# A Fourier filter and gated convolution on one core: TensorE pieces in halves of the array instead of quarters, the first input loaded whole, and a new order

## The chip, the cores and the metric

The kernel runs on one NeuronCore of a Trainium2 chip. The metric is the device time of one execution in microseconds (us). Work is done by TensorE (PE in the profile; its loads of stationary operands are the row PEld), VectorE (DVE), ScalarE (ACT) and GpSimd (POOL); SyncE (SP) and, for a few transfers at the start, ScalarE's queue issue the DMAs.

## The reference

Eight sequences x[b] of 3200 positions with 256 channels, all float32. What is computed, cut to what matters:

```python
X = np.fft.rfft(x, axis=1)                       # along the 3200 positions
Yr = Xr @ w_r - Xi @ w_i + b_r                   # complex 256x256 mix of the channels
Yi = Xr @ w_i + Xi @ w_r + b_i
Yr, Yi = soft_threshold(Yr, 0.01), soft_threshold(Yi, 0.01)
y = np.fft.irfft(Yr + 1j * Yi, n=3200, axis=1)
gate = sigmoid(sum(conv_w[k] * shifted(y, K - 1 - k) for k in range(5)))   # causal, per channel
out = (gate * (y @ w_val)) @ w_out
```

## The kernel before, in words

The transform of 3200 points is split into 64 x 50. For each of the eight sequences (`b`) there are three groups of stages.

- **First transform** (`p1`; for b = 0 `p1_first`): eight pieces `u`. A piece multiplies 50 rows of input, four quadrant matmuls of 512 columns, by the constant `f1`. Two vector operations make sum and difference, and the result goes to DRAM (`a_dram`) and comes back transposed by the load of `a`.
- **Spectrum** (`p2`, six per sequence, and `p2_last`): `s2` on TensorE (the "columns": the loaded data `a` are the stationary operand and the constant `f2`, 64 columns, streams), then casts into a high and a low part (`xs`), `mix_sum` and `mix` (float32r matmuls with 128 x 128 weights, tiles `k_ps` and `y_ps`), the threshold, and `s1i`, the first step of the transform back (`back`: constant `g1` stationary, 256 columns stream, tile `z_ps`), stored to DRAM (`z_dram`).
- **Positions and gate** (`positions`, eight per sequence): `zl` comes back from `z_dram`, `s2i` is the last step of the transform back (`zl` stationary, constant `g2` of 50 columns streams, tile `y_p`). Then `gated`: five taps of the convolution on DVE (tile `acc`), sigmoid, and the products with `w_val` (`v_ps`) and `w_out` (`o_ps`).

The three steps that the change touches are the fp32 matmuls with 64 or 50 contracted rows. Each is one call in the source and two instruction pairs in the profile (a load and a matmul, twice). The loops over `i` or `h` take the upper and the lower 64 rows of the array, and the loop over `e` takes the left and the right 64 columns: so four 64 x 64 quarters work side by side. `s2` is line 729, `s1i` line 633 and `s2i` line 819. In the profile a piece of `s2` has 64 matmul instructions (16 in each quarter), a piece of `s2i` 64 (16 in each quarter) and a piece of `s1i` 32 (8 in each quarter). There are 48, 64 and 48 such pieces.

The order of all instructions is laid out in advance on the host. `Plan.add` (line 102) takes a piece with a due key `at`, its engine and its cost in ns; `Plan.order` (line 121) plays an event model of engines, buffers (`SLOTS`), one DMA wire (`WIRE`, `BACKLOG`, `kb`) and semaphore lanes, and among the pieces that could start next on an engine takes the one with the smallest key. The offsets between stages are the numbers in `O`. Each engine then runs its instructions strictly in that order. Adjacent quarter pieces are favoured (`together`), since a change of the kind of matmul has a cost there (`SWITCH`).

At the start `p1_loads` (line 489) brings the first sequence: rows 0 to 47 of each half as one to two pieces wide, 192 or 384 KB a transfer, half 0 on SP's queue and half 1 on ACT's; rows 48 and 49 as transfers of one row each, cut in 16; the eighth piece by itself (200 KB for each half). Behind them on SP's queue come the biases, `w_r`, `w_i` and the first part of `f2` (lines 975 to 978 and 446), and behind these the stores of the first transform (`a_dram`, line 546). TensorE runs matmuls on zeros (`warm`, line 965) while it waits.

Of the kernel before, what the change touches and what calls it, by code (L numbers as in the profile page):

```python
# [18 lines left out]
P = 128  # L19
HP = P // 2  # L20
# [206 lines left out]
WIRE = 230  # L227
BACKLOG = 5000
# [7 lines left out]
def act(n, kind="copy"):  # L236
# [6 lines left out]
O = {'hold': -35.796,  # L243
     'together': 179.833,
     'later': 15.783,
     'load_x': 185.007,
     'p1': 53.805,
     'p1_step': 1.225,
     'load_a': -102.613,
     's2': -151.326,  # L250
     's1i': -39.149,
     'p3': -53.371,
     'load_z': 236.25,
     'y': 129.884,
     'conv': 171.164,
     'val': 58.845,
     'gate': 58.043,
     'project': 12.753,
     'late_val': 7.079,
     'late_out': 15.503,  # L260
     'turn': 289.535,
     'mix_sum': -73.595,
     'p1_1': -216.196,
     'load_x_1': 9.338,
     'p1_2': -26.917,
     'p3_0': -4.777}
# [9 lines left out]
def fourier_filter_then_gated_conv(ctx: ExitStack, tc: tile.TileContext, x, w_r, w_i, b_r, b_i,  # L276
# [57 lines left out]
    def load_matrix(at, name, w, dst):  # L334
        key = ("st", name)
        n = 2 * D

        def load():
            st = room(key, "o", n).rearrange("p (j d) -> p j d", j=2)
            nc.sync.dma_start(out=st, in_=w.rearrange("(j p) d -> p j d", p=P))  # L340
# [81 lines left out]
    def load_f2(at, part):  # L422
        t = slice(F2_PARTS[part] * P, F2_PARTS[part + 1] * P)
        add(at, "SP", 400, lambda: nc.sync.dma_start(out=f2_sb[:, t], in_=f2[:, t]), STORED if part else (), [("f2", part, 0)],
            kb=(t.stop - t.start) / 2)
# [12 lines left out]
    def load_bias(at):  # L438
        key = ("st", "bias")
        st = lambda: tl[key][0:1, 0:2 * D]  # L440

        def load():
            room(key, "yb", 2 * D)
            for k, b in enumerate((b_r, b_i)):
                nc.sync.dma_start(out=st()[:, k * D:(k + 1) * D], in_=b.rearrange("(o d) -> o d", o=1))
        add(-91, "SP", 800, load, (), [key + (0,)], {key: "yb"}, kb=20)

        def marks():
            nc.gpsimd.memset(f32(ones), 1.0)
# [5 lines left out]
        add(at, "ACT", act(2 * D, "cast"), lambda: nc.scalar.copy(out=rows[0:1], in_=st()), [key + (0,)], [("bias", 0, 0)])  # L455
        add(at + 0.01, "DVE", dve(2 * D), lambda: nc.vector.tensor_tensor(
            out=rows[32:33], in0=st(), in1=f32(rows[0:1]), op=ALU.subtract), [key + (0,)], [("bias", 0, 0)])
# [31 lines left out]
    def p1_loads():  # L489

        src = x[0].rearrange("(n h m) c -> h n (m c)", h=NH, m=NM)
        wide = y_sb.rearrange("p c h n -> p (c h n)")[:, 0:7 * 4 * D]
        queue = (("SP", nc.sync), ("ACT", nc.scalar))
        n = N2 - 2
        k7 = ("x", (0, 7))

        def rows(h, lo, hi):
            queue[h][1].dma_start(out=wide[h * HP:h * HP + n, lo * 4 * D:hi * 4 * D], in_=src[h, 0:n, lo * 4 * D:hi * 4 * D])

        def row(h, r):  # L500
            queue[h][1].dma_start(out=wide[h * HP + r:h * HP + r + 1, :].rearrange("p (a n) -> p a n", a=16),
                                  in_=src[h, r:r + 1, 0:7 * 4 * D].rearrange("p (a n) -> p a n", a=16))

        def single(h):
            xt = tl[k7] if h else room(k7, "x", 4 * D)
            queue[h][1].dma_start(out=xt[half(h), :], in_=src[h, :, 7 * 4 * D:])
        for i, (lo, hi) in enumerate(((0, 1), (1, 3), (3, 5), (5, 7))):
            for h in range(NH):
                add(-100 + 2 * i, queue[h][0], 400, lambda h=h, lo=lo, hi=hi: rows(h, lo, hi), (), [("x", (0, u), h) for u in range(lo, hi)], kb=130 * (hi - lo))
            if i == 0:  # L510
                for r in (n, n + 1):
                    for h in range(NH):
                        add(-99.9, queue[h][0], 400, lambda h=h, r=r: row(h, r), (), [("x_rows", (0, r), h)], kb=20)
        for h in range(NH):
            add(-93, queue[h][0], 400, lambda h=h: single(h), (), [k7 + (h,)], None if h else {k7: "x"}, kb=200)

    def p1_first(u, at):
# [29 lines left out]
        rows = [("x_rows", (0, r), h) for r in (N2 - 2, N2 - 1) for h in range(NH)] if u < 7 else []  # L547
        add(at, "PE", 890, products, [kx + (h,) for h in range(NH)] + [("f1", 0, 0), *rows], [kp + (0,), ("turn", "p1", u)], {kp: "ps_2"}, mode="q")
# [4 lines left out]
        for k in range(2):  # L553
            add(at + 0.02, "SP", 400, lambda k=k: store(k), [ks + (0,), ks + (1,)], [("a_dram", 0, (u, k)), ("stored", 0, (u, k))],
                {("a_dram", 0): "a_dram"} if (u, k) == (0, 0) else None, kb=160)

    def p1(b, u, at):
# [36 lines left out]
        add(at + O["load_x"] + O["load_x_1"] * (b == 1), "SP", 700, load, STORED if b == 1 else (), [kx + (0,)], {kx: "x"}, kb=330, chain="x", moves=2)  # L594
# [4 lines left out]
        add(at + 0.02, "SP", 1500, store, [ks + (0,), ks + (1,)], [ka + (u,)], {ka: "a_dram"} if u == 0 else None, kb=330, moves=2)  # L599
# [16 lines left out]
    def back(b, us, at, last=False):  # L616
# [5 lines left out]
        def s1i():  # L622
            p = two_banks(kz)
            if last:
                nc.tensor.matmul(p[:, 0, 0:D], g1_sb[:, 2 * us[0] * P:(2 * us[0] + 1) * P], tl[kts[0]][:, 0, :], start=True, stop=True)
                return
            for j, v in enumerate(us):
                g = g1_sb[:, 2 * v * P:(2 * v + 2) * P].rearrange("p (r q) -> p r q", r=2)

                for r in range(2):  # L630
                    for i in range(2):
                        for e in range(2):
                            nc.tensor.matmul(p[e * HP:(e + 1) * HP, i, j * D:(j + 1) * D],  # L633
                                             g[i * HP:(i + 1) * HP, r, e * HP:(e + 1) * HP],
                                             tl[kts[j]][i * HP:(i + 1) * HP, r, :], start=r == 0, stop=r == 1)
# [11 lines left out]
        def store():  # L647
# [7 lines left out]
            kb=90 * nz)  # L655
# [50 lines left out]
    def p2(b, v, at):  # L706
# [9 lines left out]
        add(at + O["load_a"], "SP", 800, load, stored_a(b), [ka + (0,)], {ka: "a"}, kb=360, chain="a", moves=2)  # L716


        def s2():
            p = buffer(k2, "ps_s2", [P, 2, 512]).rearrange("p i (j c r h k) -> p i j c r h k", j=2, c=2, r=2, h=2)  # L720
            for j, u in enumerate(us):
                for h in range(NH):
                    f = f2_sb[:, (2 * u + h) * HP:(2 * u + h + 1) * HP]
                    for c in range(2):
                        for i in range(2):
                            rows = slice(i * HP, (i + 1) * HP)
                            for e in range(2):
                                lo = c * P + e * HP
                                nc.tensor.matmul(p[e * HP:(e + 1) * HP, i, j, c, :, h, :], tl[ka][rows, h, j, lo:lo + HP],  # L729
                                                 f[rows], start=True, stop=True)  # L730
        add(at + O["s2"], "PE", 990, s2, [ka + (0,), f2_key(us[0]), f2_key(us[1])], [k2 + (0,)], {k2: "ps_s2"}, mode="q")
# [63 lines left out]
    def positions(b, k, at):  # L795
# [14 lines left out]
        def s2i():  # L810
# [4 lines left out]
            for c in range(2):  # L815
                for m in range(MB):
                    for h in range(NH):
                        for e in range(2):
                            nc.tensor.matmul(pv[h][e * HP:(e + 1) * HP, c, m, :],  # L819
                                             zt[half(h), m, c * P + e * HP:c * P + (e + 1) * HP], g2_sb[half(h), :],  # L820
                                             start=True, stop=True)
# [65 lines left out]
    def gated(b, k, at):  # L887
# [42 lines left out]
        if bk == (B - 1, NB - 1):  # L930
# [10 lines left out]
        add(kind, "SP", 400, lambda: nc.sync.dma_start(out=dst, in_=tl[ko]), [ko + (0,)], (), kb=280)  # L941
# [106 lines left out]
```

## Time and profile before

| | |
|---|---|
| median of 3 runs | 920.74 us (917.67 to 924.05) |
| the profiled execution | 926.22 us, span of its instructions 924.4 us |
| mean granted TensorE clock | 0.978 |
| TensorE matmul / weight loads busy | 868.5 us (94%) / 726.7 us (79%) |
| VectorE / ScalarE busy | 767.1 us (83%) / 591.4 us (64%) |
| DMA | 165.14 MB, mean 179 GB/s |

In rows of groups the columns are: line, engine, operation, tiles (out<-in), shape, count | busy time in us, mean ns of one | idle time of the engine just before it, with what ended it. A shape such as `64*64 64x256` is a stationary operand of 64 rows and 64 columns and 256 streamed columns. In rows of the timeline they are: start and length in us, engine, line, operation, tiles, count, and in brackets the idle time before. Ends of matmuls are modelled, so the rate of matmuls is read from their starts. "issue" is time in which an engine waited for nothing that the profile shows.

### The profile page before, as it was taken

To read this page: it belongs to the slowest core of one execution; us is meant where nothing else is said; L and a number is where in the kernel's file an instruction comes from. 1 tells how busy PE (TensorE), PEld (TensorE's weight loads), DVE (VectorE), ACT (ScalarE), POOL (GpSimd) and SP (SyncE) were. 2 spreads that over 40 slices of the span, in tenths; PEclk is the share of its full clock that TensorE was granted. 3 is DMA by queue.
4 is the path that set the end of the run, shared out by engine and by line. 5 is a ranking of instruction groups with operands and counts; after the bars stand their busy time and mean duration, and the time that the engine had idled before them with its cause. 6 is when DMAs were issued, how large, how long until landed. Compare 5 with 4: busy or idle time off the path is not lost.

```text
span 924.4 us, 29210 instructions
## 1 busy us (share of the span) xinstructions
PE 868.5 (94%) x12846; PEld 726.7 (79%) x12846; DVE 767.1 (83%) x1016; ACT 591.4 (64%) x867; POOL 5.6 (1%) x13
## 2 busy tenths in 40 slices
PE   6889889999999999899999999899999999899888
PEld 2357668879888798779878888688988998798665
DVE  1547897999889998699969998889969996798686
ACT  1235566776577776567667766576777777676553
POOL 0000000000000000000000000001000000000000
PEclk7999999999999999799999999899999999999999
DMA  7678787766464956565566475546552445323512
GB/s 142 211 233 277 245 264 235 263 202 186 130 193 145 300 175 192 164 212 176 185 222 208 144 240 183 162 166 203 163 168 98 146 143 156 110 77 117 169 54 89
DMA packets 105442, 165.14 MB, mean 179 GB/s; under 512 B 9946, under 2 KB 78172, under 8 KB 105024
## 3 DMA queue, kind: packets, MB, share of 16 engines
q1 hardware_dynamic: 104996, 161.64, 55.3%
q10 hardware_dynamic: 320, 1.64, 1.0%
q8 instruction: 101, 1.65, 0.8%
q14 instruction: 25, 0.20, 0.1%
HBM read 83.55 MB, written 79.69 MB: 177 GB/s over the span
## 4 chain that ended last, share of the span: by engine, by line
PE 67%; DVE 19%; DMA 6%; issue 5%; ACT 3%; SPq 0%; ACTq 0%; DVEq 0%
PE y_ps L768 11%; PE o_ps L851 11%; PE v_ps L851 10%; PE z_ps L633 7%; PE y_p L819 6%; PE k_ps L773 6%; DVE acc L873 6%; PE s L729 5%; PE p L572 4%; PE y_ps L766 3%; DMA zl<-z_dram 2%; DMA y_sb<-in_x 2%; PE warm L965 2%; DVE acc L915 2%; DVE gated L330 1%
## 5 line engine op out<-in xcount | busy, mean ns | idle before, releaser
L873 DVE SCALAR_TENSOR_TENSOR acc<-y_sb,cw_sb,acc 128x800 f32<-128x800 f32 (+1 forms) x264 | 259.5, 1022 | 5.6 <-ACT acc L870 4.8
L768 PE MATMUL y_ps<-w_sb,xs 128*128 128x256 f32 x1152 | 165.3, 283 | 1.0 <-issue 1.0
L851 PE MATMUL o_ps<-gated,wo_sb 128*128 128x400 f32 x756 | 152.7, 351 | 1.5 <-DVE s L585 0.8
L768 PEld LDWEIGHTS y_ps<-w_sb,xs 128*128 128x128 f32 x1152 | 152.3, 192 | 1.2 <-issue 1.1
L851 PEld LDWEIGHTS o_ps<-gated,wo_sb 128*128 128x128 f32 x756 | 136.3, 190 | 7.7 <-issue 2.0
L851 PE MATMUL v_ps<-y_hl,wv_sb 128*128 128x400 f32 x660 | 130.3, 346 | 0.5 <-ACT o L939 0.5
L851 PEld LDWEIGHTS v_ps<-y_hl,wv_sb 128*128 128x128 f32 x660 | 117.8, 188 | 1.9 <-ACT o L939 1.4
L773 PEld LDWEIGHTS k_ps<-w_sb,xs 128*128 128x128 f32 x576 | 75.7, 190 | 27.3 <-issue 15.9
L633 PE MATMUL z_ps<-tp,g_sb 64*64 64x256 f32 x1536 | 94.5, 380 | 1.3 <-issue 1.2
L773 PE MATMUL k_ps<-w_sb,xs 128*128 128x256 f32 x576 | 91.3, 294 | 1.1 <-issue 1.1
L819 PE MATMUL y_p<-g_sb,zl 50*64 50x50 f32 x4096 | 76.7, 223 | 15.8 <-issue 13.6
L819 PEld LDWEIGHTS y_p<-g_sb,zl 50*64 50x64 f32 x4096 | 69.6, 137 | 21.1 <-issue 13.5
L610 ACT ACTIVATE tp<-yb,nlam 128x512 f32<-128x512 f32 x96 | 69.8, 729 | 19.8 <-DVE yb L780 19.7
L939 ACT COPY o<-o_ps 128x800 f32<-128x800 f32 x63 | 52.0, 826 | 43.9 <-PE o_ps L851 43.1
L780 DVE TENSOR_TENSOR yb<-y_ps,kc 128x512 f32<-128x512 f32 x96 | 65.6, 683 | 17.1 <-PE y_ps L768 17.0
L328 ACT CAST gated<-acc 128x800 fp32r<-128x800 f32 x63 | 54.2, 861 | 37.6 <-DVE acc L915 37.3
L612 DVE SCALAR_TENSOR_TENSOR tp<-yb,tp 128x512 f32<-128x512 f32 x96 | 65.4, 683 | 15.4 <-ACT tp L610 15.2
L633 PEld LDWEIGHTS z_ps<-tp,g_sb 64*64 64x64 f32 x1536 | 56.8, 133 | 25.0 <-issue 6.0
L915 DVE TENSOR_TENSOR acc<-v_ps,acc 128x800 f32<-128x800 f32 x64 | 62.8, 983 | 8.3 <-PE v_ps L847 4.2
L330 DVE TENSOR_TENSOR gated<-acc,gated 128x800 fp32r<-128x800 f32 x63 | 62.0, 984 | 8.4 <-ACT gated L328 8.3
L766 PE MATMUL y_ps<-bias_rows,ones 128*128 128x256 f32 x192 | 59.4, 309 | 10.1 <-DVE yb L780 6.6
L330 DVE TENSOR_TENSOR y_hl<-y_sb,y_hl 128x800 fp32r<-128x800 f32 x55 | 54.0, 984 | 16.1 <-ACT y_hl L328 16.1
(87 smaller groups left out, 1106.6 us busy)
## 6 DMA issues: line engine op xcount, KB each, us to landing
a_dram<-s SPq DMA_DIRECT2D x128, 208.0 KB
zl<-z_dram SPq DMA_DIRECT2D x128, 200.0 KB
out<-o SPq DMA_DIRECT2D x63, 400.0 KB
a<-a_dram SPq DMA_DIRECT2D x96, 256.0 KB
z_dram<-z_t SPq DMA_DIRECT2D x48, 512.0 KB
x<-in_x SPq DMA_DIRECT2D x96, 208.0 KB
x<-in_x SPq DMA_DIRECT2D x17, 200.0 KB
y_sb<-in_x ACTq DMA_DIRECT2D x3, 384.0 KB
```

What stands on the lines that cost most here:

```text
L330: add(at + 0.001, "DVE", dve(n), lambda: nc.vector.tensor_tensor(out=low(), in0=src(), in1=f32(high()), op=ALU.subtract), [*uses, hl[0]], ...
L610: nc.scalar.activation(out=buffer(kt, "tp", [P, 2, D])[:, 0:n], in_=tl[kb][:, 0:n], func=AF.Relu, bias=nlam)
L612: add(at + 0.2, "DVE", dve(n * D), lambda: nc.vector.scalar_tensor_tensor(out=tl[kt][:, 0:n], in0=tl[kb][:, 0:n], scalar=LAM, in1=tl[kt][: ...
L633: nc.tensor.matmul(p[e * HP:(e + 1) * HP, i, j * D:(j + 1) * D], g[i * HP:(i + 1) * HP, r, e * HP:(e + 1) * HP], tl[kts[j]][i * HP:(i + 1) ...
L766: nc.tensor.matmul(p[:, 1 - r, :], ones, rows[:, (1 - r) * D:(2 - r) * D], start=True, stop=False)
L768: nc.tensor.matmul(p[:, 1 - r, :], xm(hx, j, c, r), w_sb[:, m, hw, c, :], start=False, stop=k == 5)
L773: nc.tensor.matmul(p, sm(hx, j, c), w_sb[:, 0, hw, c, :], start=k == 0, stop=k == 5)
L780: add(atu + 0.2, "DVE", dve(2 * D), lambda ky=ky, kb=kb, kc=kc: nc.vector.tensor_tensor(out=buffer(kb, "yb", [P, 2, D]), in0=tl[ky], in1=t ...
L819: nc.tensor.matmul(pv[h][e * HP:(e + 1) * HP, c, m, :], zt[half(h), m, c * P + e * HP:c * P + (e + 1) * HP], g2_sb[half(h), :], start=True ...
L851: nc.tensor.matmul(p[:, e, 0:TB], w[:, hw, c, e * P:(e + 1) * P], src(hy, c), start=n == 0, stop=n == 5)
L873: nc.vector.scalar_tensor_tensor(out=acc(c), in0=y_of(c, j), scalar=cw_sb[:, c, j:j + 1], in1=acc(c), op0=ALU.mult, op1=ALU.add)
L915: add(at + O["gate"], "DVE", dve(2 * TB), lambda: nc.vector.tensor_tensor(out=gate(), in0=hn(tl[kv][:, :, 0:TB]), in1=gate(), op=ALU.mult) ...
```

## The change

1. `s2`, `s1i` and `s2i` lose the loop over `e`: an instruction takes 64 (or 50) rows and all 128 columns, two row halves work side by side in place of four quarters, and there are half as many instructions (32, 32 and 16 a piece in place of 64, 64 and 32).
2. The first input is loaded in 16 transfers of 50 rows, 200 KB each, one for each piece and half; three of them on ACT's queue and 13 on SP's. The transfers of single rows go.
3. `w_r`, `w_i`, the biases and the first part of `f2` are moved behind the first transform's pieces on SP's queue (keys -24 to -20 and -27 in place of -90 to -88 and -91).
4. The model's costs (`WIRE`, `BACKLOG`, `kb`, `extra`, and 900 and 850 ns for `s2` and `s2i` in place of 990 and 950) and all offsets in `O` are other numbers, so that the order of all instructions is another.

```diff
-WIRE = 230
-BACKLOG = 5000
+WIRE = 210
+BACKLOG = 4000
...
-O = {'hold': -35.796,
-     'together': 179.833,
-     'later': 15.783,
-     'load_x': 185.007,
+O = {'hold': -6.037,
+     'together': 302.016,
+     'later': -48.45,
+     'load_x': 138.371,
...
-        add(-91, "SP", 800, load, (), [key + (0,)], {key: "yb"}, kb=20)
+        add(-27, "SP", 800, load, (), [key + (0,)], {key: "yb"}, kb=20, moves=2)
...
-        for i, (lo, hi) in enumerate(((0, 1), (1, 3), (3, 5), (5, 7))):
-            for h in range(NH):
-                add(-100 + 2 * i, queue[h][0], 400, lambda h=h, lo=lo, hi=hi: rows(h, lo, hi), (), [("x", (0, u), h) for u in range(lo, hi)], kb=130 * (hi - lo))
...
+        def load(u, h):
+            dst = wide[:, u * 4 * D:(u + 1) * 4 * D] if u < 7 else tl[k7] if h else room(k7, "x", 4 * D)
+            queue[h and u < 3][1].dma_start(out=dst[half(h), :], in_=src[h, :, u * 4 * D:(u + 1) * 4 * D])
+        for u in range(8):
             for h in range(NH):
+                add(-100 + u, queue[h and u < 3][0], 400, lambda u=u, h=h: load(u, h), (), [("x", (0, u), h)],
+                    {k7: "x"} if (u, h) == (7, 0) else None, kb=200)
...
-                        for e in range(2):
-                            nc.tensor.matmul(p[e * HP:(e + 1) * HP, i, j * D:(j + 1) * D],
-                                             g[i * HP:(i + 1) * HP, r, e * HP:(e + 1) * HP],
-                                             tl[kts[j]][i * HP:(i + 1) * HP, r, :], start=r == 0, stop=r == 1)
+                        nc.tensor.matmul(p[:, i, j * D:(j + 1) * D], g[i * HP:(i + 1) * HP, r, :],
+                                         tl[kts[j]][i * HP:(i + 1) * HP, r, :], start=r == 0, stop=r == 1)
...
-                            for e in range(2):
-                                lo = c * P + e * HP
-                                nc.tensor.matmul(p[e * HP:(e + 1) * HP, i, j, c, :, h, :], tl[ka][rows, h, j, lo:lo + HP],
-                                                 f[rows], start=True, stop=True)
-        add(at + O["s2"], "PE", 990, s2, [ka + (0,), f2_key(us[0]), f2_key(us[1])], [k2 + (0,)], {k2: "ps_s2"}, mode="q")
+                            nc.tensor.matmul(p[:, i, j, c, :, h, :], tl[ka][rows, h, j, c * P:(c + 1) * P],
+                                             f[rows], start=True, stop=True)
+        add(at + O["s2"], "PE", 900, s2, [ka + (0,), f2_key(us[0]), f2_key(us[1])], [k2 + (0,)], {k2: "ps_s2"}, mode="q")
...
-                        for e in range(2):
-                            nc.tensor.matmul(pv[h][e * HP:(e + 1) * HP, c, m, :],
-                                             zt[half(h), m, c * P + e * HP:c * P + (e + 1) * HP], g2_sb[half(h), :],
-                                             start=True, stop=True)
+                        nc.tensor.matmul(pv[h][:, c, m, :], zt[half(h), m, c * P:(c + 1) * P], g2_sb[half(h), :], start=True, stop=True)
...
-    load_matrix(-90, "w_r", w_r, w_sb[:, 0])
-    load_matrix(-89, "w_i", w_i, w_sb[:, 1])
-    sums(-88.9)
-    load_f2(-88, 0)
+    load_matrix(-24, "w_r", w_r, w_sb[:, 0])
+    load_matrix(-23.5, "w_i", w_i, w_sb[:, 1])
+    sums(-23)
+    load_f2(-20, 0)
     load_bias(-30)
```

More of the change, by code (lines that the diff above doesn't have):

```diff
@@ L242 @@
 T = float(NU)
-O = {'hold': -35.796,
-     'together': 179.833,
-     'later': 15.783,
-     'load_x': 185.007,
[L247 to L258, printed above, removed]
+O = {'hold': -6.037,
+     'together': 302.016,
+     'later': -48.45,
+     'load_x': 138.371,
+     'p1': 48.724,
+     'p1_step': 0.649,
+     'load_a': -101.487,
+     's2': -99.512,
+     's1i': -24.78,
+     'p3': -63.063,
+     'load_z': 121.656,
+     'y': 164.631,
+     'conv': 195.971,
+     'val': 69.272,
+     'gate': -140.59,
+     'project': 9.897,
      'late_val': 7.079,
      'late_out': 15.503,
[L261 to L266, printed above, removed]
+     'turn': 255.513,
+     'mix_sum': -0.111,
+     'p1_1': -220.218,
+     'load_x_1': 30.986,
+     'p1_2': -29.144,
+     'p3_0': 1.769}
 WARM = 6, 1, 1, 1, 1, 1, 1, 1, 14
@@ L340, in load @@
             nc.sync.dma_start(out=st, in_=w.rearrange("(j p) d -> p j d", p=P))
-        add(at, "SP", 400, load, (), [key + (0,)], {key: "o"}, kb=256)
+        add(at, "SP", 400, load, (), [key + (0,)], {key: "o"}, kb=160)
         v = lambda: tl[key][:, 0:n].rearrange("p (j d) -> p j d", j=2)
@@ L432, in load_g1 @@
         add(at, "SP", 400, lambda: nc.sync.dma_start(out=g1_sb[:, t], in_=g1[:, t]), STORED, [("g1", part, 0)],
-            kb=(t.stop - t.start) / 2)
+            kb=(t.stop - t.start) / 3.2)
     def g1_key(u):
@@ L546, in store @@
             nc.sync.dma_start(out=dst[:, :, lo:lo + 512], in_=st()[k * HP:k * HP + NF])
-        rows = [("x_rows", (0, r), h) for r in (N2 - 2, N2 - 1) for h in range(NH)] if u < 7 else []
-        add(at, "PE", 890, products, [kx + (h,) for h in range(NH)] + [("f1", 0, 0), *rows], [kp + (0,), ("turn", "p1", u)], {kp: "ps_2"}, mode="q")
+        add(at, "PE", 890, products, [kx + (h,) for h in range(NH)] + [("f1", 0, 0)], [kp + (0,), ("turn", "p1", u)], {kp: "ps_2"}, mode="q")
         first = lambda h: [START[h]] if u == 7 else []
@@ L554, in p1_first @@
             add(at + 0.02, "SP", 400, lambda k=k: store(k), [ks + (0,), ks + (1,)], [("a_dram", 0, (u, k)), ("stored", 0, (u, k))],
-                {("a_dram", 0): "a_dram"} if (u, k) == (0, 0) else None, kb=160)
+                {("a_dram", 0): "a_dram"} if (u, k) == (0, 0) else None, kb=160, extra=-300)
     def p1(b, u, at):
@@ L593, in store @@
                 nc.sync.dma_start(out=dst[:, :, lo:lo + 512], in_=st()[k * HP:k * HP + NF])
-        add(at + O["load_x"] + O["load_x_1"] * (b == 1), "SP", 700, load, STORED if b == 1 else (), [kx + (0,)], {kx: "x"}, kb=330, chain="x", moves=2)
+        add(at + O["load_x"] + O["load_x_1"] * (b == 1), "SP", 700, load, STORED if b == 1 else (), [kx + (0,)], {kx: "x"}, kb=320, chain="x", moves=2)
         add(at, "PE", 890, products, [kx + (0,), ("f1", 0, 0)], [kp + (0,)], {kp: "ps_2"}, mode="q")
@@ L598, in p1 @@
         add(at + 0.011, "DVE", dve(512), difference, [kp + (0,), ks + ("turned",)], [ks + (1,)])
-        add(at + 0.02, "SP", 1500, store, [ks + (0,), ks + (1,)], [ka + (u,)], {ka: "a_dram"} if u == 0 else None, kb=330, moves=2)
+        add(at + 0.02, "SP", 1500, store, [ks + (0,), ks + (1,)], [ka + (u,)], {ka: "a_dram"} if u == 0 else None, kb=320, moves=2, extra=-300)
     HL = ((0, 0), (0, 1), (1, 0))
@@ L715, in load @@
                 nc.sync.dma_start(out=at_[:, h], in_=src.rearrange("(j r) c -> r j c", r=P))
-        add(at + O["load_a"], "SP", 800, load, stored_a(b), [ka + (0,)], {ka: "a"}, kb=360, chain="a", moves=2)
+        add(at + O["load_a"], "SP", 800, load, stored_a(b), [ka + (0,)], {ka: "a"}, kb=320, chain="a", moves=2)
         def s2():
@@ L936, in gated @@
                     {ko: "o"} if e == 0 else None)
-                add(kind, "SP", 400, lambda e=e: nc.sync.dma_start(out=dst[:, e], in_=tl[ko][:, e]), [ko + (e,)], (), kb=140)
+                add(kind, "SP", 400, lambda e=e: nc.sync.dma_start(out=dst[:, e], in_=tl[ko][:, e]), [ko + (e,)], (), kb=125, extra=-900)
             return
@@ L940, in gated @@
             [kp + (0,), kp + (1,)], [ko + (0,)], {ko: "o"})
-        add(kind, "SP", 400, lambda: nc.sync.dma_start(out=dst, in_=tl[ko]), [ko + (0,)], (), kb=280)
+        add(kind, "SP", 400, lambda: nc.sync.dma_start(out=dst, in_=tl[ko]), [ko + (0,)], (), kb=250, extra=-900)
     def late_weights(at):
```

20 lines of the change are left out of this document (3 added, 17 removed).

## The prediction

> **What bounds the kernel now.** I read the page's busy times first, then the busy time by stage, to see where an engine has room.
>
> ```profile
> span 924.4 us, 29210 instructions
> PE 868.5 (94%) x12846; PEld 726.7 (79%) x12846; DVE 767.1 (83%) x1016; ACT 591.4 (64%) x867; POOL 5.6 (1%) x13
> ...
> PE 67%; DVE 19%; DMA 6%; issue 5%; ACT 3%; SPq 0%; ACTq 0%; DVEq 0%
> ```
>
> ```profile
> core 0: us, PE busy (x) PEld busy (x) DVE busy (x) ACT busy (x) POOL busy (x), PEclk, DMA share, GB/s
> 0.00:51.00 51.00, 38.98 (x118) 13.60 (x118) 15.65 (x24) 8.63 (x14) 1.83 (x11) 0.87 0.73 188
> 51.00:882.00 831.00, 794.34 (x12591) 688.29 (x12591) 719.16 (x951) 562.73 (x826) 3.79 (x2) 0.98 0.58 183
> 882.00:924.00 42.00, 35.18 (x140) 24.85 (x138) 32.27 (x42) 20.05 (x29) 0.00 (x0) 1.00 0.21 78
> ```
>
> All pieces that the change recuts run between 51 and 882 us. There TensorE is busy 794.3 of 831 us: it has 36.7 us to spare, and two thirds of the chain of waits is PE. What a recut piece gains or loses on PE therefore mostly reaches the end. How much of these three lines lies on the chain, its split by line tells:
>
> ```profile
> by line: PE y_ps L768 10.8%; PE o_ps L851 10.7%; PE v_ps L851 9.8%; PE z_ps L633 7.2%; PE y_p L819 6.2%; PE k_ps L773 6.0%; DVE acc L873 5.8%; issue 4.6%; PE s L729 4.5%; PE p L572 3.8%; PE y_ps L766 2.5%; DMA zl<-z_dram 2.3%; DMA y_sb<-in_
> ```
>
> **What a piece costs now.** Six groups (matmuls and loads), and one stretch of PE's timeline in which three kinds follow each other without a gap:
>
> ```profile
> L633 PE MATMUL z_ps<-tp,g_sb 64*64 64x256 f32 x1536 | 94.5, 380 | 1.3 <-issue 1.2
> L819 PE MATMUL y_p<-g_sb,zl 50*64 50x50 f32 x4096 | 76.7, 223 | 15.8 <-issue 13.6 <-DMA zl<-z_dram 1.3 <-DVE s L585 0.4
> L819 PEld LDWEIGHTS y_p<-g_sb,zl 50*64 50x64 f32 x4096 | 69.6, 137 | 21.1 <-issue 13.5 <-DMA zl<-z_dram 1.7 <-ACT y_sb L826 0.7
> L729 PE MATMUL s<-f_sb,a 64*64 64x64 f32 x3072 | 56.5, 222 | 5.0 <-ACT xs L756 3.5 <-ACT kc L778 0.7 <-issue 0.7
> L729 PEld LDWEIGHTS s<-f_sb,a 64*64 64x64 f32 x3072 | 50.4, 136 | 15.2 <-issue 4.0 <-ACT xs L756 3.6 <-DVE xs L757 1.6
> L768 PEld LDWEIGHTS y_ps<-w_sb,xs 128*128 128x128 f32 x1152 | 152.3, 192 | 1.2 <-issue 1.1
> ```
>
> ```profile
> 142.35 1.96 PE L633 MATMUL z_ps<-tp,g_sb 64*64 64x256 f32 x32
> 144.13 1.04 PE L572 MATMUL p<-x,f_sb 50*64 50x512 f32 x8
> 144.99 1.11 PE L729 MATMUL s<-f_sb,a 64*64 64x64 f32 x64
> 145.92 1.12 PE L819 MATMUL y_p<-g_sb,zl 50*64 50x50 f32 x64
> 146.97 0.97 PE L773 MATMUL k_ps<-w_sb,xs 128*128 128x256 f32 x6
> ```
>
> From start to start: s1i 144.13 - 142.35 = 1.78 us, s2 0.93 us, s2i 1.05 us (with the step to another kind of matmul behind it). Four quarters work side by side, so one quarter does s1i in 8 rounds of 222 ns, s2 in 16 rounds of 58 ns, s2i in 16 rounds of at most 66 ns. If a round were streaming alone, s1i's 222 ns for 256 columns give 0.87 ns a column: 56 ns for the 64 columns of s2, 43 ns for the 50 of s2i. s1i is bound by streaming. s2i is not; what else happens once a round in a quarter is the load of its next 64 columns, and that is my reading of its round.
>
> How long does a load take? Its recorded length holds a fixed part, so I use the difference between widths: 192 - 136 = 56 ns for 64 more columns. Taken as proportional, a load of 64 columns fills the array in 56 ns and one of 128 in 112 ns. That 56 ns is also s2's round, so it fits. Is it columns or rows that count, since the 128 x 128 load differs from the 64 x 64 one in both? Line 819 loads 50 rows and line 729 loads 64, in 137 and 136 ns: rows make no difference there. The Trainium skill, page "TensorE: Matmul & The Clock Gate", section "LDWEIGHTS (loading the stationary operand)", states this as a rule that speaks against the change: a load takes about P / 1.2 ns for P columns, however many rows; by it (an estimate) 64 columns take 53 ns and 128 take 107 ns, 54 more, and the sum below would be about 3 us smaller. The 50- and 64-row rows agree with it; no run here shows a load of 64 rows and 128 columns.
>
> **The change, part by part.**
>
> *Halves.* In s2 a row half now has 16 rounds (32 instructions on two halves), each with a load of 128 columns, so 112 ns against 56: +56 ns x 16 = +0.90 us a piece. In s2i likewise 16 rounds, +0.90 us. With 48 and 64 pieces that is 112 x 0.90 = +100 us on PE. s1i keeps 8 rounds of 222 ns, since its 112 ns load hides behind the streaming; only the first load of a piece is bare, +56 ns x 48 = +2.7 us. Bounds for the unseen 64 x 128 load: below, that it takes the 56 ns of a quarter (then nothing is added, and a round could fall from 58 to 56 ns, -3.6 us over all pieces); above, 116 ns, the spacing of the 128 x 128 loads in the second row below (0.77 us less one load's 0.192, over five steps), +108 us. I take 112, since columns and not rows moved the recorded length.
>
> ```profile
> 144.57 0.15 PEld L729 LDWEIGHTS s<-f_sb,a 64*64 64x64 f32 x4 [0.28 <-PE z_ps L633]
> 147.78 0.77 PEld L768 LDWEIGHTS y_ps<-w_sb,xs 128*128 128x128 f32 x6
> ```
>
> What of it reaches the end: the chain holds 4.5 + 6.2 = 10.7% of 924.4 us = 99 us of s2 and s2i, which last 48 x 0.93 + 64 x 1.05 = 112 us: 88%. So 0.88 x 103 = +90 us. Floor: all 36.7 us that PE spares are used up, 103 - 37 = +66 us. Ceiling: all of it in the 116 ns case, +111 us.
>
> *Start.* TensorE's first s2 begins at 51.15 us. Before it:
>
> ```profile
> 0.70:16.00 15.30, 7.67 (x12) 3.04 (x12) 0.48 (x1) 1.28 (x1) 1.19 (x6) 0.90 0.91 163
> 16.00:23.00 7.00, 6.42 (x22) 1.62 (x26) 2.77 (x4) 1.17 (x2) 0.00 (x0) 0.50 0.52 110
> ```
>
> ```profile
> 34.53 1.04 PE L527 MATMUL p<-x,f_sb 50*64 50x512 f32 x8
> 35.50 15.72 PE L965 MATMUL warm<-idle 128*128 128x512 f32 x36
> 51.15 1.04 PE L729 MATMUL s<-f_sb,a 64*64 64x64 f32 x56
> ```
>
> ```profile
> 25.74 0.62 ACT L455 CAST bias_rows<-st 1x512 fp32r<-1x512 f32 x1 [4.55 <-DMA st<-in_b_i]
> 26.26 1.05 ACT L533 COPY s<-p 128x512 f32<-128x512 f32 x2
> 36.12 1.14 ACT L328 CAST w_sb<-st 128x512 fp32r<-128x512 f32 x2
> ```
>
> ```profile
> 22.54 0.41 SPq L340 DMA_DIRECT2D st<-in_w_r  x1
> 22.99 0.47 SPq L340 DMA_DIRECT2D st<-in_w_i  x1
> 24.25 0.35 SPq L424 DMA_DIRECT2D f_sb<-in_f  x1
> 24.72 14.38 SPq L546 DMA_DIRECT2D a_dram<-s  x16
> ```
>
> ```profile
> SPq L546 <- DVE s L539: 6.4, 6, 2.0
> ```
>
> The input is 3200 x 256 x 4 bytes = 3.28 MB. At 163 GB/s it takes 20 us; at the 110 GB/s of the second stretch, my upper bound for transfers of 50 rows, 30 us. Today's last first-transform piece begins at 34.53 us, so even the slow stream needn't delay it: ScalarE stands 4.55 us for the biases at 25.74 us with the copies of the next pieces queued behind, and that wait is what the later key takes out, if the new order has it free by then. The matrices (256 KB each) leave the head of SP's queue and the stores of line 546 move up; now the matrices stand behind stores that wait for DVE (6.4 us in six waits, the last row). SP also issues 13 of the 16 input transfers itself: at the 0.35 to 0.47 us of an issue above some 5 us, beside a stream of 20 us or more. Their cover: the casts take them at 36.12 us, 13 us after the issue; if they come more than that later, ScalarE waits at line 328 and the first mix with it. I take -3 us for the start; the bounds are -5 (the whole bias wait) and +7 (all 10 us of the slower stream, less the 3 taken). The Trainium skill, page "DMA: Bandwidth & Descriptors", section "Why a DMA increments its semaphore by 16 and not by 1", has a transfer use the largest number of engines up to 16 that divides its outer size: 16 for 48 rows, 10 for 50. By it (an estimate) the stream would run at 10/16 of 163 GB/s, 102 GB/s and 32 us, near my upper bound; no row of this trace tells the engines of one transfer.
>
> *Order.* New keys move every wait between engines. The profile can't price this: 0, with 9 us to either side (a quarter of the 36.7 us that PE spares).
>
> *Sum.* 926.2 (the profiled execution) + 90 - 3 = 1013 us. That execution stands at 926.22 / 920.74 = 1.006 of the median of the runs, so against the median 1013 / 1.006 = **1007 us**. This case alone: from (926.2 + 66 - 5 - 9) / 1.006 = 972 to (926.2 + 111 + 7 + 9) / 1.006 = 1047; these ends need every bound at once, and 980 to 1035 holds most of it.
>
> **Rivals.**
>
> *The load of a half costs no more than that of a quarter* (faster, or no change). It decides at 58 ns a round: if 64 x 128 loads fill as fast as 64 x 64, because time goes by rows in steps of 64 or because both column halves are filled at once, the rounds stay as they are. In favour: a quarter's four loads do overlap (four of at least 129 ns each within 0.15 us above), so the left and the right columns can be filled together. Against: those are separate instructions, and the 128 x 128 load is 56 ns longer. Then 926.2 - 0.88 x 3.6 - 3 = 920 us, 915 against the median, 903 to 926 with the order. Chance 0.33: 0.22 faster by over 1% and 0.11 within 1%.
>
> *The instruction count is the bound* (faster). s2's 64 pairs in 0.93 us are 14.5 ns each; if that were the sequencer's pace, halving them would save 0.46 us on 112 pieces, 0.88 x 52 = 45 us: 875 us. The Trainium skill, page "TensorEngine Tiling (Array Packing)", section "Instruction Overhead", has about 60 cycles for each matmul, however few columns it streams, which would point this way. Against: the row with four loads within 0.15 us, each as long as a recorded load, has them start some 7 ns apart, so PE issues faster than 14.5 ns and then waits; and 60 cycles at any clock that gives 14.5 ns would be 4.1 GHz. Chance 0.02.
>
> *The two row halves' loads also queue behind each other.* Then 32 x 112 = 3.6 us a piece, +2.7 us x 112 x 0.88 = +263 us: 1180 us. Against: today four loads share a round. Chance 0.02.
>
> **How the numbers follow.** Forecast (loads of 128 columns bind) 0.63, rivals 0.33, 0.02, 0.02. What a measurement of this kernel can tell from no change is about 1%, so the limits are 911.5 and 929.9 us. Faster 0.22 + 0.02 = 0.24; same 0.11; slower 0.63 + 0.02 = 0.65. Cases of both signs hold much of the chance: the range runs from 903, the low end of the first rival, to 1035, and leaves out the instruction-bound case, the queued loads and the forecast's outer ends. The forecast's own range is 980 to 1035.
>
> **What would show it.** Right: groups of lines 729 and 819 with half the count, recorded loads near 190 ns, and pieces of about 1.8 us from start to start; loads busy over 79%; line 633's pieces unchanged at 1.78 us; the chain's share of PE higher, and DVE waiting for PE's `s` and `y_p`. Wrong: pieces of s2 at 0.93 us or less with half the instructions, which is the first rival; or long pieces and a span that hardly grows, which would mean that PE's place on the chain was overrated. The start is right if the first s2 begins near 48 us and ScalarE's wait at line 455 is gone.

## The result and the profile after

The changed kernel takes 1021.66 us (median of four runs, 1017.17 to 1038.65) against 922.39 us of the kernel before in the same comparison: 1.1055 of before, with a 95% interval of 1.0955 to 1.1156. It is slower by 99 us. The profiled execution of the changed kernel took 1038.65 us at a mean granted clock of 0.928; the other three, at 0.939 to 0.946, took 1017 to 1025 us, and the ratio is worked out from these three. Single figures of this trace are used for pieces, and not for the whole.

The page after, its busy times, the granted clock in 40 slices, and the chain of waits:

```profile
span 1036.7 us, 20453 instructions
PE 1015.9 (98%) x8494; PEld 878.1 (85%) x8494; DVE 773.2 (75%) x1016; ACT 602.0 (58%) x867; POOL 4.4 (0%) x13
...
PEclk9899899999999998999789998999968997599799
...
PE 95%; DVE 3%; ACT 1%; issue 0%; DVEq 0%; ACTq 0%
PE o_ps L830 14%; PE y_p L800 14%; PE y_ps L750 13%; PE v_ps L830 12%; PE z_ps L618 10%; PE s L711 9%; PE k_ps L755 8%; PE p L558 6%; PE y_ps L748 3%; PE warm L944 3%; PE v_ps L826 2%; PE p L514 1%; DVE acc L852 1%; PE y_ps L685 1%; PE y_ps L684 1%; DVE st L369 0%
```

TensorE had 94% and has 98%. DVE's 773 us and ScalarE's 602 us are nearly what they were (767 and 591). The chain went through DVE for 19% of its length before, and now for 3%; s2i and s2 hold 14% and 9% of it, where they held 6% and 5%. The clock row (a 9 stands for 0.9 and more) has more dips than the same row of the kernel before, and deeper ones late in the run, down to 0.5:

```profile
PEclk7999999999999999799999999899999999999999
```

The groups of the two steps whose round was in question (columns as before):

```profile
L800 PE MATMUL y_p<-g_sb,zl 50*128 50x50 f32 x2048 | 145.4, 303 | 0.0
L800 PEld LDWEIGHTS y_p<-g_sb,zl 50*128 50x128 f32 x2048 | 139.9, 218 | 7.2 <-issue 3.2 <-DVE acc L894 0.6 <-ACT tp L596 0.4
L711 PE MATMUL s<-f_sb,a 64*128 64x64 f32 x1536 | 101.6, 285 | 4.3 <-DVE xs L736 3.0 <-ACT s L565 1.3
L711 PEld LDWEIGHTS s<-f_sb,a 64*128 64x128 f32 x1536 | 95.7, 198 | 16.0 <-issue 5.9 <-DVE xs L736 3.3 <-ACT s L565 2.1
```

Half as many instructions keep TensorE busy for 145 us instead of 77 (s2i), and 102 instead of 57 (s2). Pieces at full clock, from PE's timeline after:

```profile
303.31 1.99 PE L800 MATMUL y_p<-g_sb,zl 50*128 50x50 f32 x32
305.24 0.38 PE L748 MATMUL y_ps<-bias_rows,ones 128*128 128x256 f32 x1
...
309.26 2.00 PE L711 MATMUL s<-f_sb,a 64*128 64x64 f32 x32
311.10 1.95 PE L618 MATMUL z_ps<-tp,g_sb 64*128 64x256 f32 x16
312.97 1.09 PE L558 MATMUL p<-x,f_sb 50*64 50x512 f32 x8
```

From start to start, s2i takes 1.93 us (1.05 before), s2 1.84 us (0.93), s1i 1.87 us (1.78). 16 rounds of 112 ns are 1.79 us.

### The profile page after: what moved, and what is told of

Read it like the earlier page. It is cut to its first block, busy times and chain, and to the rows that moved or that the text cites. A ratio compares the mean times of both kernels' runs of the same rounds, so it can differ in the third digit from the quotient of the medians.

```text
span 1036.7 us, 20453 instructions
## 1 busy us (share of the span) xinstructions
PE 1015.9 (98%) x8494; PEld 878.1 (85%) x8494; DVE 773.2 (75%) x1016; ACT 602.0 (58%) x867; POOL 4.4 (0%) x13
## 4 chain that ended last, share of the span: by engine, by line
PE 95%; DVE 3%; ACT 1%; issue 0%; DVEq 0%; ACTq 0%
PE o_ps L830 14%; PE y_p L800 14%; PE y_ps L750 13%; PE v_ps L830 12%; PE z_ps L618 10%; PE s L711 9%; PE k_ps L755 8%; PE p L558 6%; PE y_ps L748 3%; PE warm L944 3%; PE v_ps L826 2%; PE p L514 1%; DVE acc L852 1%; PE y_ps L685 1%; PE y_ps L684 1%; DVE st L369 0%
## 5 line engine op out<-in xcount | busy, mean ns | idle before, releaser
L830 PE MATMUL o_ps<-gated,wo_sb 128*128 128x400 f32 x756 | 156.6, 360 | 2.0 <-DVE acc L894 1.1
L800 PEld LDWEIGHTS y_p<-g_sb,zl 50*128 50x128 f32 x2048 | 139.9, 218 | 7.2 <-issue 3.2
L800 PE MATMUL y_p<-g_sb,zl 50*128 50x50 f32 x2048 | 145.4, 303 | 0.0
L711 PEld LDWEIGHTS s<-f_sb,a 64*128 64x128 f32 x1536 | 95.7, 198 | 16.0 <-issue 5.9
L711 PE MATMUL s<-f_sb,a 64*128 64x64 f32 x1536 | 101.6, 285 | 4.3 <-DVE xs L736 3.0
L618 PE MATMUL z_ps<-tp,g_sb 64*128 64x256 f32 x768 | 103.8, 414 | 0.0
L805 ACT COPY y_sb<-y_p 128x800 f32<-128x800 f32 x64 | 52.9, 827 | 80.2 <-PE y_p L800 80.1
L755 PE MATMUL k_ps<-w_sb,xs 128*128 128x256 f32 x576 | 97.9, 310 | 0.9 <-ACT kc L760 0.9
L755 PEld LDWEIGHTS k_ps<-w_sb,xs 128*128 128x128 f32 x576 | 83.0, 206 | 15.8 <-issue 11.4
L618 PEld LDWEIGHTS z_ps<-tp,g_sb 64*128 64x128 f32 x768 | 75.9, 202 | 17.7 <-issue 5.5
L728 ACT COPY sx<-s 128x512 f32<-128x512 f32 x48 | 28.2, 587 | 79.7 <-PE s L711 78.6
```

Of the source, the lines that this page charges most:

```text
L618: nc.tensor.matmul(p[:, i, j * D:(j + 1) * D], g[i * HP:(i + 1) * HP, r, :], tl[kts[j]][i * HP:(i + 1) * HP, r, :], start=r == 0, stop=r == 1)
L711: nc.tensor.matmul(p[:, i, j, c, :, h, :], tl[ka][rows, h, j, c * P:(c + 1) * P], f[rows], start=True, stop=True)
L755: nc.tensor.matmul(p, sm(hx, j, c), w_sb[:, 0, hw, c, :], start=k == 0, stop=k == 5)
L800: nc.tensor.matmul(pv[h][:, c, m, :], zt[half(h), m, c * P:(c + 1) * P], g2_sb[half(h), :], start=True, stop=True)
L830: nc.tensor.matmul(p[:, e, 0:TB], w[:, hw, c, e * P:(e + 1) * P], src(hy, c), start=n == 0, stop=n == 5)
```

## The experiments

The theory: a load of 128 columns takes twice as long as one of 64, whatever the number of rows, and this sets the rounds of s2 and s2i. The rivals: the new order or the new start costs the time; and, once the runs had shown it, the granted clock as a cost of its own.

**Quarters again in the changed kernel.** The three steps get back the loop over `e` (shown for s2i); the order of every engine is that of the changed kernel.

```diff
-                        nc.tensor.matmul(pv[h][:, c, m, :], zt[half(h), m, c * P:(c + 1) * P], g2_sb[half(h), :], start=True, stop=True)
+                        for e in range(2):
+                            nc.tensor.matmul(pv[h][e * HP:(e + 1) * HP, c, m, :],
+                                             zt[half(h), m, c * P + e * HP:c * P + (e + 1) * HP], g2_sb[half(h), :],
+                                             start=True, stop=True)
```

> The changed kernel with s2, s1i and s2i cut into quarters again; start and order of the changed kernel kept. If loads of 128 columns are what costs (my theory): rounds of s2 and s2i fall from 112 to 58 ns, 16 x 54 ns x 112 pieces = 97 us of TensorE time go, and the start that came some 13 us earlier stays: 900 to 920 us, clock back near 0.98. If the new order or the start costs the time (rival): above 980 us.

Measured: 903.0 us, 0.9754 of before (0.9712 to 0.9795). The halves are the whole loss, and what is left of the change is a gain. This is also a version that beats both kernels.

**Halves alone in the kernel before.**

```diff
-                        for e in range(2):
-                            nc.tensor.matmul(pv[h][e * HP:(e + 1) * HP, c, m, :],
-                                             zt[half(h), m, c * P + e * HP:c * P + (e + 1) * HP], g2_sb[half(h), :],
-                                             start=True, stop=True)
+                        nc.tensor.matmul(pv[h][:, c, m, :], zt[half(h), m, c * P:(c + 1) * P], g2_sb[half(h), :], start=True, stop=True)
```

> The kernel before with only the three steps cut into halves; its start, order and planned costs kept. Theory: +85 to +100 us from the loads, and more if the granted clock falls with them as in the changed kernel: 1005 to 1040 us. Rival (order or start): 922 us, within 1%.

Measured: 1026.8 us, 1.1055 (1.0986 to 1.1124): as much as the whole change. The granted clock was 0.933 to 0.950 in its four runs.

**The new start alone.** `p1_loads` and the keys of the biases, matrices and `f2` are those of the changed kernel.

```diff
-    load_matrix(-90, "w_r", w_r, w_sb[:, 0])
+    load_matrix(-24, "w_r", w_r, w_sb[:, 0])
...
+        for u in range(8):
             for h in range(NH):
+                add(-100 + u, queue[h and u < 3][0], 400, lambda u=u, h=h: load(u, h), (), [("x", (0, u), h)],
+                    {k7: "x"} if (u, h) == (7, 0) else None, kb=200)
```

> The kernel before with only the new start (50-row transfers, weights behind); quarters, and the same order of everything after the start. If the 13.7 us by which the first s2 came earlier reach the end: 908 us, 1.5% faster. If the earlier start is given back in later waits: 918 to 924 us.

Measured: 906.2 us, 0.9755 (0.9688 to 0.9822), the same as with quarters in the changed kernel. So with quarters no effect of the new order is seen (the intervals leave some 6 us to either side), and the start is worth 2.4%, some 20 us. The first s2 is 14 us earlier (37.10 us); what the other 6 come from was not separated, but the granted clock was 0.980 to 0.992 in these runs and 0.970 to 0.980 in the kernel before beside them.

**s2i alone in halves.**

> The kernel before with s2i alone in halves. Theory: 64 pieces x 16 rounds x 54 ns = 55 us of TensorE time, 0.88 of it on the chain: +49 us, 970 us; clock lower than 0.978 if the pieces in which the array streams least are what lowers it. Rival that s2 or s1i costs the time: within 1% of 922 us.

Measured: 982.3 us, 1.0604 (1.0503 to 1.0704), more than the loads were to cost by themselves, at a granted clock of 0.938 and 0.953. The page of this run, its clock row:

```profile
PEclk7999899999958999899979999999999996699799
```

TensorE is 97% busy in this run, and after the start none of its waits for another engine is longer than 3.5 us (the kernel with twice the streaming, below, has the same one), but the clock drops. If not gaps, what? In a round of 112 ns the array streams 50 columns, some 43 ns or 38% of the time; in the quarters' round of s2i, at most 66 ns, it was 65%.

**The same with twice the streaming.** Each s2i matmul streams its 50 columns twice; the second 50 land in columns that the next matmul overwrites, or that nobody reads. It is twice the streaming with no use, and the loads stay what they were.

```diff
-                        nc.tensor.matmul(pv[h][:, c, m, :], zt[half(h), m, c * P:(c + 1) * P], g2_sb[half(h), :], start=True, stop=True)
+                        lo = (c * MB + m) * N2
+                        g = g2_sb[half(h), :].rearrange("p (a n) -> p a n", a=1).to_broadcast([N2, 2, N2])
+                        nc.tensor.matmul(tl[kp][:, h, lo:lo + 2 * N2].rearrange("p (a n) -> p a n", a=2),
+                                         zt[half(h), m, c * P:(c + 1) * P], g, start=True, stop=True)
```

> The kernel before with s2i alone in halves, as in the run of s2i alone, but each s2i matmul streams its 50 columns twice (100 columns, the second 50 go into columns that the next matmul overwrites or that nobody reads). At full clock 100 columns take 87 ns, still under the 112 ns load, so a round stays 112 ns. If the clock is lowered because the array streams so little of the time in these pieces: the granted clock goes back to 0.97 or more and the kernel gets faster than the run with 50 columns, 1.06 to 1.02-1.045 of before, although it streams twice as much. Rival, the clock is lowered by something else (loads, gaps, the length of pieces): clock near 0.94 and 1.06 or slower.

Measured: 946.8 us, 1.0239 (1.0197 to 1.0282), clock 0.987 in every run. The clock row, one piece of the timeline, and the group of the loads:

```profile
PEclk7999899999999999999999999999999999999999
```

```profile
401.61 2.03 PE L820 MATMUL y_p<-g_sb,zl 50*128 50x100 f32 x32
403.58 1.96 PE L633 MATMUL z_ps<-tp,g_sb 64*64 64x256 f32 x32
```

```profile
L820 PEld LDWEIGHTS y_p<-g_sb,zl 50*128 50x128 f32 x2048 | 118.1, 188 | 7.8 <-ACT y_hl L328 1.5 <-DVE acc L915 0.6 <-issue 0.6
```

The piece is about as long as with 50 columns (1.97 against 1.93 us), so the load still binds, and the kernel is 36 us faster for streaming columns that nobody needs. Loads, instruction count and length of the piece stay, so it is the longer streaming that brings the clock back. What exactly is counted, the share of time or something that goes with it, is not shown.

That the 36 us are the clock's, time times clock tells. The runs of the kernel before beside these experiments, 33 of them at clocks of 0.970 to 0.987, give 897 to 908 us for this product, 902 in the mean: in these runs the time goes as one over the clock. s2i in halves gives 928 and 929 us, and with twice the streaming 934 to 935 us. At the same clock the longer streams win nothing.

**All halves, with longer streams, three ways.** s2i as above, and every second s2 matmul streams 128 columns (the next one overwrites half of them). First with the start and order of before:

```diff
+                            to, w = (p[:, i, j, c, :, h, :], f[rows])
+                            if h == 0:
+                                to = p[:, i, j, c, :, :, :]
+                                w = f[rows].rearrange("p (r o k) -> p r o k", r=2, o=1).to_broadcast([HP, 2, 2, NM])
+                            nc.tensor.matmul(to, tl[ka][rows, h, j, c * P:(c + 1) * P], w, start=True, stop=True)
```

> The kernel before with halves in all three steps (1.106 of before by themselves), in which s2i streams its 50 columns twice and every second s2 matmul 128 columns instead of 64 (the extra columns are overwritten by the next matmul); 87 and 109 ns stay under the 112 ns of a load. If the granted clock follows the share of time in which the array streams: clock 0.97 or more, rounds still 112 ns, and only the cost of the loads is left: 1.05 to 1.07 of before, 970 to 988 us. If the loads alone make up the whole loss and the clock is a by-product: 1.10 or more.

Measured: 983.7 us, 1.0673 (1.058 to 1.0767), clock 0.989. With the clock at 0.989 the halves cost 6.7%; without the longer streams, 10.6%. But 0.989 is more than the kernel before had beside it (0.972 to 0.987). By time times clock, 973 us here against 902, the halves cost about 70 us at equal clock. The busy time of this run by stage (columns as in the prediction):

```profile
0.00:52.00 52.00, 39.48 (x118) 13.79 (x118) 15.66 (x24) 8.63 (x14) 1.82 (x11) 0.87 0.75 186
52.00:942.00 890.00, 880.25 (x8238) 785.86 (x8238) 726.97 (x952) 572.53 (x826) 3.51 (x2) 1.00 0.53 170
942.00:984.00 42.00, 35.33 (x140) 25.11 (x138) 31.72 (x41) 19.69 (x28) 0.00 (x0) 0.99 0.21 78
```

Between the first s2 and the last s2i, TensorE's busy time grew from 794.3 to 880.3 us, by 86 us, and the stretch from 831 to 890 us, by 59: the other 27 us went into TensorE's idle time, which fell from 36.7 to 9.7 us. The clock of the stretch is mixed into both: it was 0.98 before and is 1.00 here.

Second, the changed kernel with the same streams, so with its own start and order:

> The changed kernel with the same longer streams in s2i and in every second s2 matmul; its start and order kept. If with the clock held up the new start is worth its 2.4% again and the new order costs nothing, as it did with quarters: 1.025 to 1.045 of before, about 20 us under the run with the order and start of before. If the new order is bad for halves as such, whatever the clock: no better than that run, 1.05 to 1.07.

Measured: 980.1 us (976.8 to 983.0), 1.0634 (1.0552 to 1.0716), not the 1.025 to 1.045 hoped for from the start: its gain is missing here too, with the clock at 0.987 to 0.994. Its stages:

```profile
0.00:36.00 36.00, 33.75 (x118) 12.54 (x118) 15.75 (x24) 9.04 (x14) 1.82 (x11) 1.00 0.68 223
36.00:934.00 898.00, 884.81 (x8231) 787.78 (x8230) 724.05 (x951) 570.37 (x825) 2.54 (x2) 0.99 0.53 171
934.00:979.00 45.00, 37.63 (x148) 26.84 (x148) 32.82 (x42) 21.32 (x29) 0.00 (x0) 0.98 0.20 73
```

The start is 16 us shorter, the middle 8 longer, the tail 3 longer. Third, to separate start and order, the new start with the order of before:

> Halves with the longer streams and the new start, in the order of before: between the two last kernels (1.067 with the start and order of before, 1.063 with those of the change; first s2 at 52.3 and 36.4 us). If the new order gives back what the start wins once TensorE has no slack: about 15 us under the kernel without the new start, 1.045 to 1.052. If the start itself is worth little in halves: 1.060 to 1.067.

Measured: 970.3 us (969.1 to 972.6), 1.0608 (1.0528 to 1.0688), its profiled execution at a clock of 0.996. Its stages:

```profile
0.00:36.00 36.00, 33.68 (x117) 12.45 (x118) 15.63 (x24) 8.94 (x14) 1.82 (x11) 1.00 0.69 226
36.00:925.00 889.00, 879.32 (x8234) 785.14 (x8233) 726.17 (x951) 571.43 (x825) 3.50 (x2) 1.00 0.54 172
925.00:968.00 43.00, 36.17 (x150) 25.71 (x146) 32.20 (x41) 20.32 (x29) 0.00 (x0) 1.00 0.21 77
```

The ratios of the three overlap. The expectation had 1.045 to 1.052 if the new order gives the start's gain back, and 1.060 to 1.067 if the start itself is worth little; the ratio falls into the second. But the kernel before ran at 911 to 929 us in these comparisons, following its own clock, and blurs the ratios. The stages are clearer: with the order of before the middle is 889 us, as without the new start (890), and the 16 us of the start reach the end. With the new order the middle is 898 us. So, as far as three profiles tell, the new order is 9 us worse in the middle and some 2 in the tail when the pieces are halves. Where the middle loses can be seen between 100 and 160 us; the order of the change is the first row, that of before the second:

```profile
100.00:160.00 60.00, 50.34 (x478) 43.74 (x476) 42.44 (x84) 26.22 (x44) 0.00 (x0) 0.89 0.60 184
100.00:160.00 60.00, 56.53 (x597) 46.70 (x597) 47.03 (x88) 34.63 (x58) 0.00 (x0) 1.00 0.78 253
```

TensorE is idle for 9.7 us instead of 3.5 (it waits for DVE 3.6, 3.1 and 2.5 us at a time), and its clock in this stretch is 0.89 instead of 1.00, some 6 us more. Which of the order's moves brings these waits is not settled.

**Halves and the new start without the longer streams.** The same question at the lowered clock:

> The kernel before with halves in all three steps and with the new start; the order of everything after the start, and the planned costs, are those of before. Halves alone gave 1.106 of before, the start alone 0.976, the whole change 1.106 again. If the new order is what eats the start's gain once halves are in: 1.08 of before, 1000 us. If an earlier start is worth nothing once TensorE is the only bound, or the clock eats it: 1.10 to 1.11.

Measured: 1009.8 us, 1.0887 (1.0801 to 1.0973). It lies between the two expectations, 17 us under halves alone; its interval just touches that of the whole change and not that of halves alone. The whole change takes 12 us more, the same way as the stages above. Time times clock lies between 961 and 964 us in all runs of both, so here the whole difference stands in the clock (0.943 to 0.962 in this kernel, 0.928 to 0.946 in the changed one).

**What makes the start shorter: the transfers without the moved weights.** 50-row transfers as in the change; biases and matrices keep their keys.

> The kernel before with only the 50-row transfers of 200 KB (13 on SP's queue, 3 on ScalarE's); the biases and matrices keep their keys ahead of the first transform's stores. If the transfers themselves carry the gain of the start: first s2 near 40 us and 908 to 914 us. If moving the weights carries it: first s2 near 48 us and 918 us or more.

Measured: 910.3 us, 0.9833 (0.9779 to 0.9887), first s2 at 42.02 us.

**And 48-row transfers made narrow.** Two queues and single rows stay; each transfer is one piece wide.

```diff
-        for i, (lo, hi) in enumerate(((0, 1), (1, 3), (3, 5), (5, 7))):
+        for i, (lo, hi) in enumerate((u, u + 1) for u in range(7)):
```

> The kernel before with the input still in 48-row transfers on two queues and single rows, but each transfer one piece wide (4 KB a row, 192 KB) instead of two. If the 8 KB rows and waiting for 384 KB at a time made the input slow: input at 200 GB/s or more instead of 163, first s2 near 42 us, 910 to 914 us. If 48 rows, single rows or two queues are what is slow: 163 GB/s, first s2 near 50 us, within 1% of before.

Measured: 917.4 us, 0.996 (0.992 to 0.9999), first s2 at 45.49 us, between the two expectations. The first s2 comes at 51.15, 45.49, 42.02 and 37.10 us in the kernel before, with narrow 48-row transfers, with 50-row transfers, and with the weights behind as well: about 6, 3 and 5 us. The timelines show where the time goes. Before, ScalarE, its queue and the first products:

```profile
1.98 4.51 ACTq L498 DMA_DIRECT2D y_sb<-in_x  x3
13.12 0.29 ACTq L506 DMA_DIRECT2D x<-in_x  x1
13.44 1.28 ACT L533 ACT_TABLE_LOAD   x1 [13.44 <-DMA y_sb<-in_x]
16.58 3.94 PE L527 MATMUL p<-y_sb,f_sb 50*64 50x512 f32 x16 [7.46 <-DMA y_sb<-in_x]
18.81 0.59 ACT L533 COPY s<-p 128x512 f32<-128x512 f32 x1 [4.09 <-PE p L527]
```

With narrow 48-row transfers:

```profile
1.98 12.38 ACTq L498 DMA_DIRECT2D y_sb<-in_x  x6
12.59 3.26 PE L527 MATMUL p<-y_sb,f_sb 50*64 50x512 f32 x16 [3.07 <-DMA y_sb<-in_x]
15.21 0.29 ACTq L506 DMA_DIRECT2D x<-in_x  x1
15.54 1.28 ACT L533 ACT_TABLE_LOAD   x1 [15.54 <-DMA y_sb<-in_x]
16.83 1.07 ACT L533 COPY s<-p 128x512 f32<-128x512 f32 x2
```

With 50-row transfers:

```profile
0.73 1.30 ACTq L498 DMA_DIRECT2D y_sb<-in_x  x3
2.06 1.28 ACT L520 ACT_TABLE_LOAD   x1 [2.06 <-issue]
8.82 1.95 PE L514 MATMUL p<-y_sb,f_sb 50*64 50x512 f32 x16
```

With the new start alone, the first and the last piece of the first transform:

```profile
9.12 1.95 PE L514 MATMUL p<-y_sb,f_sb 50*64 50x512 f32 x16
20.43 1.09 PE L514 MATMUL p<-x,f_sb 50*64 50x512 f32 x8 [0.24 <-issue]
```

Before, the first product waits for its input until 16.58 us. ScalarE stands behind its own input transfers until 13.44 us, but is then ready before the product: its first copy waits 4.09 us for it. With narrow transfers the first product begins at 12.59 us, and now ScalarE, free only at 16.83 us, is 2 to 3 us late (an estimate: the eight matmuls of a piece last 1.1 us at full clock and some 2 at half). With only three transfers on its queue it is free at some 3 us, after its table load. The last piece of the first transform begins at 34.53 us before and at 20.43 us with the new start, 14.1 us earlier, which is all that the first s2 gains; 7.5 us of it stand already at the first piece. How much comes from 50 rows, from narrow transfers, from the single rows that go, or from the queue was not separated.

## Why the prediction was right, point by point

The forecast was 1007 us, slower; measured 1021.66 us. The direction, the mechanism and its place hold. The sizes of the terms don't hold as well as their sum.

- **The round: right.** 112 ns predicted for a load of 128 columns; pieces of 1.84 and 1.93 us from start to start, and recorded loads at 188 ns where the clock is full (the group of the run with twice the streaming), near the 192 of the 128 x 128 loads before. Rows don't count: 64 rows and 128 columns cost as much as 128 and 128.
- **s1i: right.** 1.87 us against 1.78; its longer first load is all that shows.
- **"88% of it reaches the end": wrong.** With the longer streams, TensorE's 86 us became 59 us, 69%. At equal clock it is about 70 us of the 104 us that the pieces add (0.91 us x 48, 0.88 us x 64 and 0.09 us x 48), also two thirds. The step read the chain's share as if the chain could not move. What happened is what the floor of that step described: TensorE's idle time was used up, 27 of 36.7 us. The floor, 66 us, was the better estimate of this term than the 90 us that were taken.
- **The clock: a term that was missing.** The prediction took 0.978 as given. Halves alone give 1.1055 of before; at equal clock, by time times clock (969 against 902 us), they would give 1.074. The rest, some 3% or 30 us, is the lowered clock. It is chance that this and the step above nearly cancel: +90 and 0 were predicted, about +70 and +30 measured.
- **The start: wrong in size.** -3 us were taken, with -5 as the bound; the first s2 came at 37.46 instead of 51.15 us, and with quarters the gain was 2.4%, some 20 us. The step priced ScalarE's wait for the biases alone, since even a slow stream need not delay the last piece at 34.53 us. It passed over the first product, which waited 7.46 us for its input; with the new start the last piece came at 20.43 us. The rate of the input, which the step took as the limit, hardly changed. Until 10 us hardly anything but input moves, before (first row) and with the start alone (DMA share and rate in the last two columns):

```profile
0.70:10.00 9.30, 7.67 (x12) 3.04 (x12) 0.48 (x1) 0.00 (x0) 1.19 (x6) 1.00 0.92 170
0.70:10.00 9.30, 8.54 (x20) 3.49 (x24) 0.48 (x1) 1.28 (x1) 1.19 (x6) 1.00 0.58 161
```

  By the Trainium skill's page "DMA: Bandwidth & Descriptors", section "Why a DMA increments its semaphore by 16 and not by 1", 50 rows go on 10 engines and 48 on 16, and the estimate by it was 102 GB/s. The busy share fits that, 0.58 against 0.92, a ratio of 0.63; the estimate does not come out, with 161 GB/s for 50 rows and 170 for 48. The trace does not show the engines of one transfer.
- **The order: 0, with 9 us to either side.** With quarters no difference (0.9754 against 0.9755). With halves some 11 us worse, by the stages of three profiles, about half of it idle time of TensorE and half the lower clock beside it.
- **The rivals.** Loads of a half as cheap as of a quarter: fell with the round. Instruction count as the bound: fell, since half the instructions took twice the time. Loads of the two row halves behind each other: fell, as that would be 3.6 us a piece.

The sum by measured terms, an estimate: 922 + 70 (loads) - 14 (start) + 6 (the idle time of the order) = 984 us at the clock of before, 0.978. At 0.943, the mean of the three runs at 0.939 to 0.946, it is 984 x 0.978 / 0.943 = 1020 us, so the clock adds some 36 us; these runs took 1017 to 1025 us.

## What to carry to other kernels

Before you merge small matmuls into larger ones, compare the load of the stationary operand with the streaming, round by round: four quarters load two times 64 columns side by side, and merging them makes one load of 128, which, by an estimate from these pieces, binds as soon as fewer than 128 or so columns stream in fp32 (112 ns at 0.87 ns a column). Then look at what the merged piece does to the granted clock. And an engine whose queue also issues transfers is not free until they are issued (13.44 us with seven, 2.06 us with three): see whether its first work is due before that. Here it cost 2 to 3 us in one run, and nothing in the kernel before, where the input itself came later.

## What the runs showed of the hardware that was not expected

TensorE's granted clock can fall to one half although the engine has work without a gap; in the rows below it does so where the array streams only a small part of the time. PE's timeline after, from 866 us, where pieces of s2i and s2 follow each other closely, and the busy time from 870 to 887 us, in which the clock was 0.51:

```profile
866.52 3.78 PE L800 MATMUL y_p<-g_sb,zl 50*128 50x50 f32 x64
870.23 1.46 PE L755 MATMUL k_ps<-w_sb,xs 128*128 128x256 f32 x6
871.62 3.68 PE L711 MATMUL s<-f_sb,a 64*128 64x64 f32 x32
875.09 3.60 PE L800 MATMUL y_p<-g_sb,zl 50*128 50x50 f32 x32
878.63 4.37 PE L830 MATMUL o_ps<-gated,wo_sb 128*128 128x400 f32 x12
882.92 3.66 PE L800 MATMUL y_p<-g_sb,zl 50*128 50x50 f32 x32
```

```profile
870.00:887.00 17.00, 17.00 (x122) 16.03 (x121) 5.53 (x7) 6.90 (x10) 0.00 (x0) 0.51 0.22 70
```

Two s2i pieces run at full clock (3.71 us from start to start for both), and after them s2 takes 3.47 us instead of 1.84, s2i 3.54 instead of 1.93, and even the twelve `o_ps` matmuls 4.29 us, 357 ns each, where the mean of one is 207 in the whole run (156.6 us for 756, the group below): matmuls and loads both at half speed. No idle time stands in these rows.

```profile
L830 PE MATMUL o_ps<-gated,wo_sb 128*128 128x400 f32 x756 | 156.6, 360 | 2.0 <-DVE acc L894 1.1 <-ACT o L918 0.9
```

The Trainium skill, page "TensorE: Matmul & The Clock Gate", section "HAM oscillation — how this bites in real kernels", gives the rule that there should be no idle gap of TensorE over some 3.4 us; here there is no gap, so avoiding gaps is not enough. Streaming the 50 columns twice brought the clock from 0.938 and 0.953 to 0.987, and the kernel from 982 to 947 us.
